# A windowed attention with an expert layer behind it: VectorE's operations between two SBUF tiles given to other engines, with a new list of steps

## The chip, the core and the metric

The kernel runs on one core of a Trainium2 chip. A core has TensorE (PE in the profile; its weight loads are PEld), VectorE (DVE), ScalarE (ACT), GpSimd (POOL) and SyncE (SP), which issues most DMAs. The metric is device time in microseconds (us), the median of several executions.

## The reference: what is computed

Two layers follow each other for a batch of 8 sequences of 576 tokens.

```python
# attention: 8 heads of 64, a symmetric window of 32 tokens on each side
scores = scale * np.matmul(q, k.transpose(0, 1, 3, 2))
mask = np.abs(pos[:, None] - pos[None, :]) <= window
scores = np.where(mask, scores, -1000000000.0)
...
x = softmax(scores) @ v            # heads side by side: (8, 576, 512)
# experts: 4 causal attention heads of 64, each with its own wq, wk, wv, wo
logits = x @ w_gate                # the 2 largest of 4, softmax over them: w
ye = softmax(causal(scale * (x @ wq[e]) @ (x @ wk[e]).T)) @ (x @ wv[e]) @ wo[e]
out = sum over the 2 chosen experts of w * ye
```

The inputs q, k and v are float32; the kernel computes the first layer's products in float32 and most of the second in bfloat16.

## The kernel before, in words

The work is a list of 967 steps, the string ORDER, written out in one line of text after another. A loop at the end of the kernel takes them one by one and calls the function of that name. The instructions of each engine run in the order of the list; between engines only data and buffers order them. A step is written as name and numbers, then after a colon the engine (v VectorE, g GpSimd, a ScalarE; for products of PE, p is whole and q is in halves of 64 rows of the result), then after @ the PSUM banks. So mk2011:g is the mask product of batch 2, group 0, half 1, pair 1, on GpSimd.

The steps of the first layer, by batch b and group g of four heads:

- lq, lk, lv load q, k and v. Each load is made to wait for the last PE instruction ahead of it in the list.
- tq and tk (line 317) turn q and k into tile T on VectorE, by a stream transpose from SBUF to SBUF. The first loads go another way: hq and hk turn them on PE, and iq and ik copy the result from PSUM into T.
- qc and kc copy one part of T to another place in T (line 184 when on VectorE or GpSimd, line 182 when on ScalarE), and mv moves further parts by four DMAs. There are 12 of each of the three: this doubles the rows of a product of q and k.
- sc multiplies q and k (line 190), ex takes the exponential out of PSUM into tile A (ScalarE, line 418), and mk multiplies A by the window's mask, tile MASKP (line 422). For batch 0 the mask is added on PE instead and there is no mk, so there are 56 mk steps.
- vc copies parts of v inside tile V. av multiplies A and V into PSUM, and un (lines 450 to 457, VectorE) divides into tile XN.
- xt turns XN on PE (line 193), xf copies that out of PSUM to XTF and xb casts XTF to XTB in bfloat16, both tiles in SBUF.

The steps of the second layer, by batch b and pair j of experts:

- ga, gt, ge, gm, gu compute the gate's weights (PE, then VectorE in lines 529 to 551, with one exponential on ScalarE).
- pp and pe compute q and k of the experts and cast them out of PSUM to QKE; pv and ve do this for v (VE).
- ps multiplies, xe takes the exponential into ATE (ScalarE, lines 618 and 620), se sets what is not causal to zero (GpSimd, line 623).
- po multiplies with v, oe (lines 657 to 659, VectorE) divides, applies the gate and writes OE; pt turns OE on PE (line 193), ot copies it to OTT.
- py multiplies with wo, ye copies to Y, st stores. For the last batch's last pair, pw, ow, tw and uw do po to ot in three parts.

lw0 to lw3 load the weights wq, wk, wv and wo, and cw0 to cw3 cast them. s_mask and s_nb build the masks at the start. The names after an arrow in the profile are tiles: A<-A,MASKP is a mask product, T<-T a qc or kc (or, as a DMA, an mv), XTB<-XTF an xb.

Tiles are few: A has three sets, T and V two each, XTF one, QKE and ATE three, OE two. A step that writes a tile waits until the readers of its last content are done.

Of the kernel before, what the change touches and what calls it, by code (L numbers as in the profile page):

```python
# [39 lines left out]
    lv23 un11@3 lq300:e av10@0 un10@0 cw2:a ex1111@5 mk1111:g pv01@7 lk300:e ve01:a@7 sc200@24 ex2001@4 ex2000@2  # L40
    sc201@06 ex2011@6 ex2010@0 tq210:e ps001:p@4 tk210:e xe001@4 xt10@2 lk310:e se013 mk1110:g xf10:a@2 ps000:p@6
    xe000@6 kc21:g lv20 av12@0 un12@0 av13@4 ps012:p@2 xe012@2 se001 un13@4 av14@0 un14@0 tq300:e qc21:g mv21
    ps002:p@6 lw3 xt11@4 xe002@6 se002 lv22 xf11:a@4 xt12@2 xf12:a@2 xb10:g xb12:g xb11:a pv00:p@0 ps003:q@4 ga1@2
    mk2010:g tk300:e ve00:a@0 xe003@4 lv21 se003 gt1 ge1 pp100:p@6 gm1 mk2001:g pe100:a@6 gu1@2 pp101:p@4
# [3 lines left out]
    ot01:v@7 pt00@6 xe100@0 pv10:p@4 ve10:v@4 ot00:a@6 lv31 mk2100:g ps113:p@0 ps110:p@2 xe113@0 mk2101:g xe110@2  # L48
    sc300@06 ex3000@0 sc301@24 ex3001@6 ex3010@2 pv11@0 py02@1 se101 ve11:a@0 ex3011@4 lq410:e vc21:g qc31:g
    ps112:p@6 mk2011:v xe112@6 mk2110:g vc20:g lv33 se103 av23@2 tq400:e un23@2 py01:q@4 se102 kc31:a mv31  # L50
    ps111:q@6 xe111@6 ye01:a@4 ye02:a@1 st02 tk400:e kc40:a se113 av24@0 se100 po10@2 oe10@2 mk3001:g av22@6 se110
    py00:q@4 pt10@3 qc40:a un24@0 st01 un22@6 ot10:v@3 se112 se111 po11@0 oe11@0 av20@6 ye00:a@4 st00 mk3010:g
    av21@4 un20@6 pt11@0 ot11:a@0 un21@4 mv40 sc310@26 ex3100@2 mk3011:g mk3000:v mk3100:g lk500:e sc311@04
    tq410:e ex3101@6 ex3110@0 ex3111@4 py11:q@2 lq500:e lv30 py12@7 ye12:a@7 xt20@0 ye11:a@2 xt21@4 lv32 xf21:a@4
    mk3111:g qc41:g py10:q@6 xf20:v@0 xb20:g xb21:g xt22@2 xf22:v@2 lv34 ye10:a@6 lv41 xb22:a sc401@04 ex4010@0
    mk4010:g tk410:e lv44 lk510:e sc400@26 ex4011@4 ex4000@2 pp200:q@0 pp201:q@2 ex4001@6 pp210:q@6 tk500:e
    pe200:a@0 pp211:q@0 pe201:a@2 kc41:a pe210:a@6 ga2@2 vc31:a mk3110:g ps202:p@6 tq500:e gt2 gm2 ps200:p@3
    pe211:a@0 mk3101:g av34@5 vc30:g av32@0 un34@5 ge2 gu2@2 un32@0 mk4011:g xe202@6 se202 mv41 xe200@3 qc50:a
    lq510:e av31@6 av30@2 pv21@0 un31@6 kc50:g mv50 mk4001:g ve21:a@0 av33@4 xt32@6 xf32:a@6 un30@2 mk4000:g lv43
    lv40 un33@4 xb32:a sc410@02 ex4101@2 sc411@46 mk4101:v lk600:e ex4100@0 tk510:e ex4111@6 mk4111:g xt30@2  # L60
    xf30:a@2 xt31@0 pv20:q@6 ve20:v@6 xf31:a@0 ex4110@4 lv42 ps212:q@0 xe212@0 sc501@24 ex5010@2 ex5011@4 lq600:e
    xb30:g mk4110:g sc500@06 xb31:g mk5010:g ex5000@0 ps211:q@2 xe211@2 pp300:p@4 lq610:e tq510:e pe300:v@4
    pp301:p@0 ex5001@6 ps203:q@2 ps201:q@4 lk610:e pe301:a@0 xe203@2 xe201@4 tk600:e qc51:g ga3@7 ps213:p@2
    xe213@2 ps210:p@0 ps302:p@5 xe210@0 xe302@5 gt3 kc51:g pp311:q@2 vc41:g pe311:a@2 vc40:g av43@0 mv51 pv31@6
# [24 lines left out]
    py42@6 ps601:q@4 st32 ps511:q@2 av74@7 un74@7 xe511@2 xe601@4 se601 av71@0 ye42:a@6 se511 un71@0 pp610:q@2
# [695 lines left out]
```

## Time and profile before

| | before |
|---|---|
| median of 3 runs | 252.7 us (249.24, 252.70, 253.34) |
| the profiled execution | 247.55 us |
| its span, first to last instruction | 245.7 us |
| mean granted clock of PE | 0.985 |
| DMA | 47.69 MB, mean 194 GB/s |

The profile is of one execution. Busy times of the engines overlap; a share of busy time is an average over stages with different limits. A row of a group ends with the idle time that its engine had just before these instructions and what ended it. In the timeline a row gives start, length, engine, line, operation, tiles and count; runs of equal instructions are merged into one row, and a bracket names the idle time ahead of it with what ended that. A row of a window gives its bounds, its length, the busy time of PE, PEld, DVE, ACT and POOL with their counts of instructions, the granted clock, the share of the DMA engines and GB/s.

### The profile page before, as it was taken

How to read it: one execution, taken by the hardware profiler on the slowest of the kernel's cores; microseconds unless marked ns; L12 is line 12 of the kernel's file. 1: busy time of each engine (PE TensorE's matmuls, PEld its weight loads, DVE VectorE, ACT ScalarE, POOL GpSimd, SP SyncE). 2: the span in 40 equal slices, each digit the busy share in tenths (PEclk: the TensorE clock that was granted, in tenths of full speed). 3: DMA queues.
4: the chain of work that ended last, by engine and by line, in shares of the span. 5: the costliest groups of instructions: out<-in, count | busy, mean ns of one | idle time of the engine just before them, and what ended most of it. 6: DMA issues, size and time to landing. Idle time of an engine off the chain costs nothing. (4 is left out here: it accounts for less than half of the span.)

```text
span 245.7 us, 11651 instructions
## 1 busy us (share of the span) xinstructions
PE 220.3 (90%) x5104; PEld 174.9 (71%) x5104; DVE 184.4 (75%) x326; ACT 165.6 (67%) x258; POOL 149.6 (61%) x195
## 2 busy tenths in 40 slices
PE   7989699999919999998998998999998799799991
PEld 3978576877806787987886876878786578567750
DVE  2551999799997998995896699877999776356651
ACT  2556268698815959986986895678658446677762
POOL 7003189648926956983998789298989623522310
PEclk9999999999976999999999999999999999999999
DMA  6889978898948689999997995894641403014555
GB/s 226 248 208 308 312 207 243 224 303 205 200 103 287 175 227 277 239 244 230 245 271 167 250 214 188 191 232 109 187 149 55 127 20 109 4 54 151 184 195 193
DMA packets 57107, 47.69 MB, mean 194 GB/s; under 512 B 40416, under 2 KB 42976, under 8 KB 57056
## 3 DMA queue, kind: packets, MB, share of 16 engines
q1 hardware_dynamic: 56480, 45.76, 68.1%
q10 hardware_dynamic: 576, 1.18, 1.3%
q8 instruction: 40, 0.66, 1.2%
q14 instruction: 11, 0.09, 0.1%
HBM read 30.42 MB, written 9.44 MB: 162 GB/s over the span
## 5 line engine op out<-in xcount | busy, mean ns | idle before, releaser
L422 POOL TENSOR_TENSOR A<-A,MASKP 128x576 f32<-128x576 f32 x46 | 65.5, 1435 | 12.6 <-ACT A L418 12.1
L618 ACT ACTIVATE ATE<-PS 128x1024 bf16<-128x1024 f32 x48 | 47.8, 1028 | 11.7 <-PE PS L190 11.4
L623 POOL TENSOR_SCALAR_AFFINE_SELECT ATE<-ATE 128x256 bf16<-128x256 bf16 (+1 forms) x80 | 29.8, 398 | 37.3 <-ACT ATE L618 28.3
L418 ACT ACTIVATE A<-PS 128x576 f32<-128x576 f32 x64 | 38.2, 654 | 12.6 <-PE PS L190 11.9
L190 PE MATMUL PS<-V,A 128*64 128x65 f32 (+1 forms) x1280 | 41.1, 223 | 2.4 <-issue 1.6
L190 PEld LDWEIGHTS PS<-V,A 128*64 128x64 f32 (+1 forms) x1280 | 37.0, 132 | 7.3 <-issue 3.7
L190 PE MATMUL PS<-T 64*64 64x128 f32 (+7 forms) x1440 | 39.5, 264 | 1.4 <-ACT XTF L182 0.6
L317 DVE STREAM_TRANSPOSE T<-kn 128x1152 f32<-128x1152 f32 x14 | 32.4, 2327 | 7.8 <-DMA kn<-in_k_dram 6.6
L190 PEld LDWEIGHTS PS<-T 64*64 64x64 f32 (+1 forms) x1440 | 33.7, 132 | 4.7 <-ACT XTF L182 0.8
L317 DVE STREAM_TRANSPOSE T<-qn 128x1152 f32<-128x1152 f32 x14 | 32.6, 2331 | 4.0 <-PE PS L190 3.1
L184 POOL COPY V<-V 64x2048 f32<-64x2048 f32 (+1 forms) x14 | 25.0, 1788 | 15.3 <-DMA V<-in_v_dram 14.2
L184 POOL CAST XTB<-XTF 128x1024 bf16<-128x1024 f32 (+1 forms) x25 | 16.5, 682 | 13.8 <-ACT XTF L182 12.8
L190 PE MATMUL PS<-QKE 64*64 64x64 bf16 (+9 forms) x252 | 18.9, 287 | 4.9 <-DVE OE L659 2.6
L451 DVE TENSOR_TENSOR XN<-PS,RC 128x512 f32<-128x512 f32 x32 | 22.1, 691 | 1.2
L182 ACT COPY XTF<-PS 128x1024 f32<-128x1024 f32 (+1 forms) x20 | 16.4, 828 | 9.6 <-PE PS L193 5.7
L182 ACT CAST QKE<-PS 128x576 bf16<-128x576 f32 x26 | 16.6, 643 | 7.8 <-PE PS L190 7.8
L190 PE MATMUL PS<-WV,XTB 128*128 128x256 bf16 (+2 forms) x208 | 19.8, 265 | 1.1 <-DVE XN L451 1.1
L182 ACT COPY Y<-PS 128x1024 f32<-128x1024 f32 (+1 forms) x20 | 16.2, 825 | 6.2 <-PE PS L190 3.6
L190 PE MATMUL PS<-WO,OTT 128*128 128x512 bf16 (+2 forms) x116 | 19.2, 352 | 0.7 <-DVE G L551 0.4
L190 PE MATMUL PS<-XTB,WQ 128*128 128x288 bf16 (+1 forms) x168 | 18.5, 287 | 0.1
L190 PE MATMUL PS<-XTB,WK 128*128 128x288 bf16 (+1 forms) x168 | 18.1, 287 | 0.0
L190 PEld LDWEIGHTS <-XTB 128*128 128x128 bf16 (+1 forms) x208 | 15.4, 107 | 3.6 <-issue 1.7
(88 smaller groups left out, 321.3 us busy)
## 6 DMA issues: line engine op xcount, KB each, us to landing
V<-in_v_dram SPq DMA_DIRECT2D x32, 256.0 KB, 5.4
out_dram<-Y SPq DMA_DIRECT2D x16, 512.0 KB, 3.9
qn<-in_q_dram SPq DMA_DIRECT2D x28, 288.0 KB, 4.6
kn<-in_k_dram SPq DMA_DIRECT2D x28, 288.0 KB, 5.0
T<-T SPq DMA_DIRECT2D x48, 144.0 KB, 4.3
V<-in_v_dram SPq DMA_DIRECT2D x8, 128.0 KB, 5.2
out_dram<-Y SPq DMA_DIRECT2D x16, 64.0 KB, 2.5
qn<-in_q_dram SPq DMA_DIRECT2D x2, 320.0 KB, 4.7
```

Source lines behind the costliest of these rows:

```text
L182: nc.scalar.copy(o, i)
L184: eng(c).tensor_copy(o, i)
L190: last_pe[0] = nc.tensor.matmul(*a, **kw)
L317: nc.vector.transpose(T.rearrange("q h (p o) -> q h o p", o=18)[:, :, o0:o1, :], x[:, :, o0:o1, :])
L418: nc.scalar.activation(AT[(2 * b + g) % NAT_][half][p], two(b0)[:, :, 0:HS], EXP, scale=scale_att)
L422: eng(c).tensor_tensor(out=ap, in0=ap, in1=MASK[:, None, HS * half:HS * half + HS].to_broadcast([128, 2, HS]), op=MULT)
L451: nc.vector.tensor_tensor(out=XN[T // 2][:, T % 2, :].rearrange("p (t h d) -> p h t d", t=4, h=8), in0=u[:, :, 0:64].rearrange("p h (d t) ...
L618: nc.scalar.activation(chunk(A, ch), two(b0), EXP, scale=scale_moe)
L623: nc.gpsimd.affine_select(ap, ap, pattern=[[0, n], [1, w]], compare_op=IS_GE, fill=0.0, base=0, channel_multiplier=-1)
```

## The change

The list of steps is replaced by another with the same 967 names. No function changes. In the new list no mk, qc, kc, vc, xb or cw step has the letter v:

| steps | before: v, g, a | after: v, g, a |
|---|---|---|
| mk | 10, 46, 0 | 0, 56, 0 |
| qc | 2, 7, 3 | 0, 8, 4 |
| kc | 0, 5, 7 | 0, 6, 6 |
| vc | 0, 14, 2 | 0, 13, 3 |
| xb | 1, 19, 4 | 0, 18, 6 |
| cw | 0, 2, 2 | 0, 3, 1 |
| iq and ik | 1, 0, 7 | 4, 0, 4 |
| xf | 7, 0, 17 | 10, 0, 14 |
| pe | 6, 0, 26 | 10, 0, 22 |
| ve | 5, 0, 11 | 7, 0, 9 |
| ot and uw | 9, 0, 9 | 8, 0, 10 |
| ye | 4, 0, 20 | 5, 0, 19 |

The stream transposes tq and tk and the mask set-up s_nb stay on VectorE. Steps in halves (q): pp 10 before and 12 after, ps 20 and 22, py 5 and 3, pv 1 and 0. The order and the banks of nearly all steps differ too, so the diff of the text is the whole string. Parts of it that the prediction speaks of:

```diff
-    lq001:e s_fill wm3@0 wm2@0 lq002:e s_warm s_ident lk001:f lq012:e lk002:f lk012:f lk011:f s_ones lv00 hq000@0
...
-    tq100:e lw1 hq010@0 iq010:a@0 lk100:e tk100:e lw0 hk010@4 cw0:g ik010:a@4 sc011@02 ex0110@0 sc010@46 lk110:e
...
-    pp011:p@4 pe011:a@4 lq210:e lw2 mk1000:g tq200:e qc20:g sc110@02 ex1100@0 ex1101@2 tk200:e kc20:a mk1010:g
...
-    pe101:a@4 lq310:e sc210@06 sc211@24 ex2101@6 kc30:g qc30:v mv30 ex2100@0 ex2110@2 se000 se011 pp110:q@6 se010
-    ex2111@4 lq400:e tk310:e se012 po01@2 oe01@2 pe110:a@6 ps103:p@4 cw3:a xe103@4 ps102:p@6 xe102@6 lk400:e
-    po00@0 pp111:p@4 oe00@0 mk2000:g lk410:e pe111:a@4 pt01@7 mk2111:g ps101:q@2 ps100:q@0 xe101@2 tq310:e
...
-    xe402@2 se303 mk5110:g av54@4 gm4 gu4@5 av53@0 un54@4 un53@0 qc70:g mv70 lk710:e av52@2 lv72 un52@2 xf50:a@6
...
-    xf62:v@2 ex7111@4 xb62:g xt60@6 xf60:v@6 xb60:v ex7110@0 xt61@4 xf61:a@4 sc710@02 ex7101@2 vc70:g xb61:g
+    lq012:e s_fill wm2@0 s_ones wm3@0 lk001:f lk002:f lq002:e lv03 lq001:e lk012:f s_ident hq011@0 iq011:v@0 lv00
+    hk000@7 ik000:a@7 s_mask s_nb lk011:f hk001@2 lk100:e ik001:a@2 hq001@0 lq011:e hq000@2 hk011@3 lv01 ik011:a@3
+    lv02 vc00:g lw2 iq001:v@0 iq000:v@2 sc001@06 sc000@24 tk100:e s_warm ex0011@6 ex0000@2 ex0010@0 hk010@6
...
+    tk200:e kc20:g xb00:a cw1:a lv14 lv10 ex1010@0 pp010:p@2 pe010:a@2 lv13 qc20:a pp011:p@4 pe011:a@4 lk210:e
...
+    pe111:a@2 pp110:p@0 se012 se001 po00@4 ps103:q@2 pe110:a@0 xe103@2 se010 mk2010:g tq300:e qc30:g mv30
+    ps102:q@0 xe102@0 lk400:e lv24 tk310:e kc31:a lq400:e po01@6 oe00@4 ps100:p@2 ps101:p@0 xe100@2 pv10:p@4 lv31
...
+    sc300@02 tk400:e ex3011@6 ex3010@4 py00:q@6 ex3000@0 vc21:g ex3001@2 mk2111:g mk2110:g av23@4 un23@4 ps113:q@2
...
+    se110 un24@7 se112 se111 vc30:a ye01:a@0 se113 po11@2 oe11@2 av21@4 un21@4 av20@0 un20@0 pt10@7 pt11@6 kc40:a
...
+    xt21@6 xf20:v@4 xb20:g py10:p@0 ye11:a@2 xf21:a@6 xb21:g xt22@2 sc401@46 ye10:a@0 ex4010@4 ex4011@6 xf22:v@2
+    sc400@02 xb22:a ex4000@0 lv34 lv41 mk3110:g qc41:g lv42 tk410:e tk500:e ga2@4 gt2 ex4001@2 pp200:q@6 lv43
...
+    tk510:e kc51:g pp300:p@6 pe300:v@6 vc40:g ex5000@0 mk5000:g pp301:p@2 pe301:a@2 tq600:e tk600:e
...
+    sc711@04 ex7110@0 st21 lv74 se501 ex7111@4 mk7001:g xt62@6 xf62:v@6 xt61@2 xf61:v@2 xt60@0 xf60:a@0 sc710@46
...
```

More of the change, by code (lines that the diff above doesn't have):

```diff
@@ L40 @@
[L40 to L44, printed above, removed]
@@ L50 @@
[L50 to L54, printed above, removed]
@@ L55 @@
[L55 to L64, printed above, removed]
@@ L95 @@
-    ps702:p@2 xe703@4 xe702@2 ps700:p@6 xe700@6 py51:p@4 pt60@0 ot60:a@0 st41 ye51:a@4 se611 po61@2 oe61@2 st52
-    st50 ga7@7 ps701:p@0 ps712:p@2 xe701@0 gt7 ge7 gm7 gu7@7 pt61@4 se703 ot61:a@4 xe712@2 st51 pv70:p@5 se701
-    py60:p@0 ye60:a@0 se702 py61:p@3 ye61:a@3 st60 st61 se712 ve70:v@5 pw710@7 ow710@7 se700 po70@5 py62@0 oe70@5
-    pw711@7 ow711@7 ps713:q@3 xe713@3 se713 ye62:a@0 st62 tw710@1 pt70@2 ot70:v@2 tw711@0 uw710:a@1 py70:p@1
-    uw711:a@0 py71:p@6 ye70:a@1 st70 ye71:a@6 pw712@0 st71 ow712@0 tw712@0 uw712:a@0 py72@0 ye72:a@0 st72
+    lq012:e s_fill wm2@0 s_ones wm3@0 lk001:f lk002:f lq002:e lv03 lq001:e lk012:f s_ident hq011@0 iq011:v@0 lv00
@@ new lines @@
+    sc100@46 xb01:g ex1001@6 ex1000@4 lv12 mk1001:g tq110:e sc101@02 tq200:e ex1011@2 wm1@7 mk1000:g mk1011:g
+    tk200:e kc20:g xb00:a cw1:a lv14 lv10 ex1010@0 pp010:p@2 pe010:a@2 lv13 qc20:a pp011:p@4 pe011:a@4 lk210:e
+    sc110@06 ga0@2 ex1101@6 gt0 mk1101:g ps010:q@6 gm0 pp000:p@4 pv01@3 pe000:v@4 ve01:v@3 ex1100@0 mk1100:g
+    vc10:g mv20 xe010@6 ge0 vc11:a gu0@2 lq210:e sc111@06 ex1111@6 tk210:e mk1111:g ex1110@0 mk1110:g kc21:g lv23
+    pp001:p@4 pe001:a@4 av10@2 un10@2 lv21 ps003:p@4 ps000:p@0 xe000@0 av11@6 lw3 un11@6 se000 ps011:p@2 xe003@4
@@ new lines @@
+    sc200@04 mk1010:g xe011@2 se011 ex2000@0 sc201@26 lk300:e lq300:e ex2001@4 mk2001:g ex2010@2 ps002:q@0 xe002@0
+    ex2011@6 tq210:e qc21:g mv21 av13@4 un13@4 av12@2 lv20 ps012:p@0 ps001:p@4 un12@2 xe012@0 av14@6 xe001@4
+    xt10@2 un14@6 se003 ps013:p@0 xe013@0 xt11@6 mk2000:g xf10:v@2 lk310:e xb10:g xt12@4 lv22 xf11:a@6 xb11:a
+    pv00:p@0 ve00:a@0 xf12:v@4 tk300:e kc30:a lv32 ga1@7 gt1 gm1 ge1 xb12:g pp100:q@5 pe100:a@5 se013 pp101:q@0
+    pe101:a@0 gu1@7 se002 sc211@24 ex2110@2 lq310:e sc210@06 cw3:g ex2100@0 mk2011:g ex2101@6 pp111:p@2 ex2111@4
@@ new lines @@
+    ex4110@4 lk600:e xt31@2 xf31:a@2 mk4110:g lv44 xb31:g tq510:e se200 qc51:g ex4111@6 pv20:p@0 ve20:v@0
+    ps212:q@2 xe212@2 sc501@46 ex5010@4 mk4111:g ex5011@6 vc41:g sc500@02 ex5001@2 lk610:e lq610:e ps211:q@4
+    xe211@4 tk510:e kc51:g pp300:p@6 pe300:v@6 vc40:g ex5000@0 mk5000:g pp301:p@2 pe301:a@2 tq600:e tk600:e
+    ps201:p@4 xe201@4 qc60:g ps203:p@0 xe203@0 ga3@7 gt3 se203 ps302:p@2 ps213:p@4 ps210:p@0 mk5001:g xe213@4
+    se213 pv31@6 pp311:q@4 xe302@2 xe210@0 mv51 av43@2 un43@2 av42@0 pe311:a@4 ge3 kc60:a mv60 ve31:a@6 pp310:q@4
@@ new lines @@
+    se300 mk5100:g po21@6 oe21@6 xe311@2 pp411:p@4 pp401:p@2 vc51:g qc70:a qc61:g pe411:v@4 ga4@0 pe401:a@2
+    ps403:p@4 ps401:p@6 kc61:a xe403@4 se403 ps310:p@1 xe401@6 mv61 xe310@1 pv41@3 tk700:e av51@4 lv61 av50@6
+    pt21@1 lv71 pt20@2 ot20:a@2 kc70:a st11 un51@4 ot21:a@1 gt4 un50@6 ve41:v@3 pv40:p@4 ge4 gm4 gu4@0 xt50@2
+    ps402:p@6 ve40:a@4 xe402@6 mk5111:g mk5011:g av54@1 mk6010:g av53@4 av52@6 xf50:a@2 un54@1 un53@4 ps313:q@2
+    mk6000:g mk6011:g xe313@2 xb50:g mv70 un52@6 sc610@04 st10 ex6100@0 sc611@26 tq710:e ex6101@4 se311 pp410:p@0
@@ new lines @@
+    av60@0 un61@3 ge5 gu5@2 un60@0 pe510:a@6 av63@6 un63@6 av62@2 pp511:q@0 un62@2 av64@7 pe511:a@0 mk7010:g
+    un64@7 ps410:q@2 xe410@2 mv71 lv70 sc711@04 ex7110@0 st21 lv74 se501 ex7111@4 mk7001:g xt62@6 xf62:v@6 xt61@2
+    xf61:v@2 xt60@0 xf60:a@0 sc710@46 ex7101@6 ex7100@4 se410 se413 ps412:q@2 pv50:p@0 xe412@2 se400 py20:p@4
+    ye20:a@4 se402 mk7000:g py31:p@2 ve50:v@0 po40@0 oe40@0 mk7111:g xb60:a ga6@4 ps500:p@5 ye31:a@2 xe500@5 gt6
+    ps510:p@0 xe510@0 gm6 se412 se411 po41@2 pt40@7 mk7100:g oe41@2 st22 xb61:g xb62:g pp601:p@5 pe601:v@5 ge6
@@ new lines @@
+    se512 se502 po50@4 oe50@4 se602 st31 xe611@0 py41:p@2 xb70:g ye41:a@2 st41 py40:p@6 ye40:a@6 ps610:p@0
+    ps612:p@4 se600 st40 se510 po51@2 xe610@0 oe51@2 xe612@4 xb72:g xb71:g pp711:p@6 pp710:p@0 pp700:p@4 pe710:v@0
+    se611 pe711:a@6 pe700:v@4 pt50@7 se601 ot50:a@7 pt51@0 se612 ot51:a@0 po60@2 oe60@2 ps613:q@4 xe613@4
+    ps711:q@6 ps710:q@0 xe711@6 xe710@0 se711 pp701:q@4 pe701:v@4 pv71@7 py52@6 se610 py50:q@2 st42 ye52:a@6
+    ve71:v@7 st52 ye50:v@2 ps703:q@4 st50 xe703@4 ps702:q@0 ps701:q@6 xe702@0 py51:p@4 ye51:v@4 se613 xe701@6
@@ L100 @@
+    po61@2 st51 ps712:p@0 oe61@2 xe712@0 se712 ps700:p@6 xe700@6 se700 se702 ga7@4 pt61@3 pt60@2 gt7 se701
+    ot60:a@2 se710 ge7 ot61:a@3 pv70:p@0 gm7 py60:p@2 py61:p@6 ye60:a@2 ve70:v@0 pw710@5 gu7@4 ow710@5 se703
+    po70@0 py62@2 oe70@0 ps713:q@4 st60 ye61:a@6 pw711@3 ow711@3 pt70@0 ye62:a@2 ot70:v@0 tw710@6 uw710:a@6
+    tw711@3 st61 uw711:v@3 py70:p@0 st62 xe713@4 py71:p@4 ye70:a@0 st70 ye71:a@4 st71 se713 pw712@7 ow712@7
+    tw712@7 uw712:a@7 py72@7 ye72:a@7 st72
 """
```

64 lines of the change are left out of this document (27 added, 37 removed).

## The prediction

> **What bounds the kernel now.** I read the page's head first, then PE's own waits, then the timeline around the two longest of them, then the groups of VectorE (DVE) and GpSimd (POOL).
>
> ```profile
> span 245.7 us, 11651 instructions
> PE 220.3 (90%) x5104; PEld 174.9 (71%) x5104; DVE 184.4 (75%) x326; ACT 165.6 (67%) x258; POOL 149.6 (61%) x195
> ...
> PEclk9999999999976999999999999999999999999999
> ```
>
> PE is busy 220.3 of 245.7 us, so what can be won by reordering is the other 25.4 us and whatever the low clock in slices 12 and 13 cost. PE's waits, longest first (total, times, longest):
>
> ```profile
> PE PS L193 <- DVE OE L659: 5.1, 1, 5.1
> PE PS L190 <- issue: 3.2, 4, 1.0
> PE PS L190 <- DVE OE L659: 2.6, 1, 2.6
> ```
>
> Two single waits, both for VectorE's OE, are 7.7 us. The timeline shows what VectorE did before them. First one:
>
> ```profile
> 61.67 7.97 DVE L184 COPY T<-T 128x576 f32<-128x576 f32 x1
> 62.01 1.84 POOL L623 TENSOR_SCALAR_AFFINE_SELECT ATE<-ATE 128x256 bf16<-128x256 bf16 x5
> 63.82 5.50 POOL L422 TENSOR_TENSOR A<-A,MASKP 128x576 f32<-128x576 f32 x4
> 69.56 2.32 DVE L317 STREAM_TRANSPOSE T<-kn 128x1152 f32<-128x1152 f32 x1
> 72.19 0.82 DVE L659 TENSOR_TENSOR OE<-PS,RG 128x640 bf16<-128x640 f32 x1
> 73.07 0.72 PE L193 MATMUL PS<-ident_bf,OE 128*128 128x128 bf16 x5 [5.09 <-DVE OE L659]
> 73.72 1.19 PE L190 MATMUL PS<-QKE 64*64 64x448 bf16 x12
> 75.34 3.09 PE L190 MATMUL PS<-WV,XTB 128*128 128x256 bf16 x16
> ```
>
> The copy of step qc30:v is on VectorE from 61.67 to 69.64, as long as POOL has selects and mask products queued back to back (62.01 to 69.32), and ends 0.3 us after the last of them. The transpose and two OE groups stand behind it; PE stands still for 5.09 us and then runs at half clock:
>
> ```profile
> 71.00:72.00 1.00, 0.00 (x0) 0.00 (x0) 0.96 (x3) 0.00 (x0) 0.00 (x0) 0.50 1.03 235
> 76.00:77.00 1.00, 1.00 (x6) 0.75 (x5) 0.74 (x2) 0.93 (x2) 0.97 (x1) 0.50 0.93 277
> ```
>
> (One-microsecond windows; the third figure from the end is the granted clock, 0.50.) The second wait follows a VectorE cast between two SBUF tiles (xb60:v), a third, smaller one a second T copy (qc61:v):
>
> ```profile
> 185.64 5.26 DVE L184 CAST XTB<-XTF 128x1024 bf16<-128x1024 f32 x1
> 187.22 2.78 POOL L422 TENSOR_TENSOR A<-A,MASKP 128x576 f32<-128x576 f32 x2
> 192.15 0.41 PE L190 MATMUL PS<-QKE 64*64 64x512 bf16 x4 [2.60 <-DVE OE L659]
> ...
> 150.10 2.37 DVE L184 COPY T<-T 128x576 f32<-128x576 f32 x1
> 153.37 1.91 PE L190 MATMUL PS<-WV,XTB 128*128 128x256 bf16 x16 [1.09 <-DVE XN L451]
> ```
>
> The same kinds of work on the engines that take them over, and VectorE's mask products (the last two rows give min/median/max in ns):
>
> ```profile
> L422 POOL TENSOR_TENSOR A<-A,MASKP 128x576 f32<-128x576 f32 x46 | 65.5, 1435 | 12.6 <-ACT A L418 12.1
> L184 POOL COPY T<-T 128x576 f32<-128x576 f32 x12 | 8.1, 686 | 3.8 <-DVE RC L450 2.7 <-DVE T L317 1.0
> L182 ACT CAST XTB<-XTF 128x1024 bf16<-128x1024 f32 x2 | 2.1, 1041 | 0.0
> L422 DVE TENSOR_TENSOR A<-A,MASKP 128x576 f32<-128x576 f32 x10 | 11.6, 1165 | 2.7 <-ACT A L418 2.7
> ...
> L422 DVE TENSOR_TENSOR A<-A,MASKP x10: 749/908/2249, 39.0 to 193.4; 128x576 f32<-128x576 f32 x10
> L422 POOL TENSOR_TENSOR A<-A,MASKP x46: 1396/1416/1947, 34.6 to 196.8; 128x576 f32<-128x576 f32 x46
> ```
>
> So a bound of PE, with holes that VectorE makes while it waits beside POOL.
>
> **The change part by part.** The program builds every computing instruction as before; engines, PSUM banks, halves (p or q) and places move.
>
> 1. *Off VectorE:* ten mask products (11.6 us), two T copies (7.97 and 2.37), one XTB cast (5.26): 27.2 us. *Onto VectorE, out of PSUM:* four iq evictions for one ik, four pe casts (0.758 each below) and five more small evictions on balance, about 9.6 us by the rows of VectorE's PSUM copies. VectorE ends near 184.4 - 27.2 + 9.6 = 167 us. ScalarE loses about 5 us; it is under 70% busy and ends no long wait of PE: nothing on the path.
>
> ```profile
> L184 DVE CAST QKE<-PS 128x576 bf16<-128x576 f32 x6 | 4.5, 758 | 3.7 <-PE PS L190 3.7
> L182 ACT CAST QKE<-PS 128x576 bf16<-128x576 f32 x26 | 16.6, 643 | 7.8 <-PE PS L190 7.8
> ```
>
> 2. *What of that is on the path.* The first wait: 5.09 us still, and after it work at half clock. The 16 matmuls of pv10 take 3.09 us there and 1.91 us at 153.37: 1.2; the ten of pt (0.72 us twice) and the twelve of ps (1.19) lose about 1.0 of their 2.63 by the same ratio: 7.3 us in all. The second wait 2.60, the third 1.09. Together 11.0 us. With the T copy gone the transpose starts at 61.7 and the OE groups find their matmuls done late (po01 begins at 65.9), so next in line is PE itself. I take all 11.0 as won; the bounds are 3.7 (only the two later waits go) and 11.0.
>
> 3. *Onto POOL:* ten products at 1.416 = 14.2, one more qc and kc each (0.67), one V copy and one XTB cast fewer, WV and WO's casts for WK's: about +13.9, to 163.5 us, 69% of a 236 us span. Spread out that is nothing; it isn't spread. From step se010 (PE's po00) to vc40 (before av43) the new list gives POOL 21 products (29.7), 8 T copies (5.3), 3 long and 2 short V copies (9.1), 11 wide and 2 narrow selects (5.2), 3 wide XTB casts and one pair of narrow ones (3.7): 53.0 us. The unit costs, and PE's work between the same steps in the trace:
>
> ```profile
> L184 POOL COPY V<-V 64x2048 f32<-64x2048 f32 x7 | 13.7, 1953 | 14.5 <-DMA V<-in_v_dram 14.2
> L184 POOL COPY V<-V 64x1536 f32<-64x1536 f32 x7 | 11.4, 1623 | 0.8 <-issue 0.7
> L623 POOL TENSOR_SCALAR_AFFINE_SELECT ATE<-ATE 128x256 bf16<-128x256 bf16 x64 | 25.4, 424 | 30.1 <-ACT ATE L618 28.3 <-issue 1.8
> L184 POOL CAST XTB<-XTF 128x1024 bf16<-128x1024 f32 x13 | 13.5, 1039 | 13.1 <-ACT XTF L182 12.8
> ...
> 65.91:126.21 60.30, 54.15 (x1254) 43.23 (x1254) 51.77 (x70) 43.79 (x72) 43.70 (x44) 0.94 0.84 222
> ```
>
> (In the 60.30 us from po00 to av43 PE was busy for 54.15 and POOL for 43.70.) Less the 2.2 of half clock, PE needs 52 us: POOL is full where it had air. At se010 the new list has POOL about 3 us ahead of PE (its work there waits only for xf12 and then runs through), and following the queues by the rows above, mk2110 is ready about 3 us before av23 needs it, se113 under 1 us before po11, xb21 about when pp200 starts, vc40 under 1 us before av43. Behind a late product stand selects and V copies, and for each of them PE. I charge 1.5 us; the bounds are 0 and a repeat of the first wait (7.3) at each of the three batches in the stretch, 21.9.
>
> 4. *Start.* WV's load (lw2) now goes out before WQ's and WK's, and V's block 3 before q's second part.
>
> ```profile
> Y<-in_moe_wv_dram SPq DMA_DIRECT2D x1, 512.0 KB, 6.9
> 24.00:30.00 6.00, 4.07 (x121) 3.40 (x120) 5.68 (x11) 1.00 (x3) 1.17 (x2) 1.00 1.07 309
> ```
>
> The queues are full then (share 1.07 at 309 GB/s), so 512 KB ahead of WK's load move that by 1.7 us. cw1 is on ScalarE's queue and pp011, pe010 and the exponentials of sc101 wait behind it. Against that PE's small waits for V and XN at 24 to 30 (1.9 us idle) are dealt anew. I charge +1.0, bounds -1 and +3.
>
> 5. *The rest of the list.* PE's other idle time is 25.4 - 5.09 - 2.60 - 1.09 = 16.6 us, much of it at start and end, which keep their shape (the last block is still pw712 to st72). The order of nearly every step differs, SP's too, where mv and the loads stay in pairs with their turns and place. I take the same 16.6 and give it 3 us either way. p and q halves cost the same: 16 half matmuls of pp 1.17 us, 8 whole ones 1.14.
>
> ```profile
> 63.43 1.17 PE L190 MATMUL PS<-XTB,WQ 128*64 128x288 bf16 x16
> 66.84 1.14 PE L190 MATMUL PS<-XTB,WK 128*128 128x288 bf16 x8
> ```
>
> Sum: -11.0 + 1.5 + 1.0 = -8.5 us. The profiled execution took 247.55 us (span 245.7), and would become 239.0. The median of the runs shown is 252.7 (249.24 to 253.34), 5.15 above the profiled one; I carry the difference over: 252.7 - 8.5 = 244.2 us.
>
> **The rivals.**
>
> *POOL gives the gain back in part.* One or two waits like item 3's bound. For: POOL's 53 us in 52. Against: most of its 61% share has idle time ended by ScalarE, not by itself. Two of 7.3: 252.7 - 11.0 + 14.6 = 256.3; one: 249.0. Within 2%.
>
> *POOL becomes the bound (other side).* In each of the batches 2, 3 and 4 PE waits for the mask product or the select of a queue that has lost its lead, long enough that the clock halves as it did at 71.00 (after about 3 us of standing). Three times 7.3 = 21.9, 252.7 - 11.0 + 21.9 = 263.6. It decides from the third such wait; two are not enough. For: the same full stretch; a product costs 1.4 on POOL and 0.75 on a free VectorE (the two rows of min/median/max). Against: in the stretch as I follow it nothing is over 1 us late. The Trainium skill, GPSIMD Engine Reference, Key points, has the rule that speaks for this rival: elementwise work is structurally about twice as fast on VectorE. By that rule ten products should not go to POOL at all; the trace agrees on the price, 0.749 against 1.396 us at the least.
>
> *The long copy is chance.* A blocked VectorE instruction gets in after one POOL instruction in most executions, and the 7.97 is an accident of this one. Then only 3.7 is won: 252.7 - 3.7 + 2.5 = 251.5. Against: 5.26 and 2.37 are over the copy's usual cost too, and the runs without a profile are longer, not shorter. The Trainium skill, SBUF — State Buffer, Who interferes with whom, has this rule: of a VectorE copy in a two-port mode and a GpSimd instruction, whoever issues first gets the shared ports for the whole instruction, and the other blocks. Taken at its word the copy waits for one instruction; in this trace it waited for ten.
>
> *The change does not do what it says.* Stream transposes still go from SBUF to SBUF on VectorE. They show no such wait:
>
> ```profile
> L317 DVE STREAM_TRANSPOSE T<-qn x14: 2316/2332/2341, 14.8 to 160.9; 128x1152 f32<-128x1152 f32 x14
> ```
>
> Fourteen within 25 ns, with POOL busy beside many; no chance of its own.
>
> **How the numbers follow.** 2% (5.05 us, about what a measurement of this kernel can tell from no change) puts the bounds at 247.65 and 257.75. The forecast, 244.2, has 0.62, its own range 236 to 247.6: below, all 11.0 won with no charge and no gap between profile and median (247.55 - 11.0 = 236.5); above, a charge of 6. POOL gives it back in part 0.13, the long copy is chance 0.07: both within 2%, 0.20. POOL the bound 0.18, slower. The range 236 to 257.7 holds all but that last case.
>
> **What would show it.** Right: no VectorE COPY, CAST or product with SBUF source other than the transposes and the mask set-up; VectorE near 167 us busy and POOL near 163; no wait of PE for OE over 2 us; PEclk 9 throughout; PE idle near 16 to 19 us. Item 3 wrong: PE waits ended by POOL A, POOL ATE or POOL V of over 1 us between 60 and 120 us. Item 4 wrong: ScalarE's WK cast ended by a DMA wait of over 2 us, with PE idle near 35 us. The forecast is wrong if the PEclk row shows a new dip.

## The result and the profile after

| | before | after |
|---|---|---|
| median of 4 runs | 250.97 us (248.91 to 253.34) | 237.19 us (234.73 to 238.82) |
| the profiled execution | 247.55 us | 234.73 us |
| its span | 245.7 us | 233.0 us |

The ratio is 0.949 [0.9351, 0.9629], and 0.9529 [0.9455, 0.9603] in a second measurement on another chip. Ratios here are of undisturbed executions only (within 1.5% of the fastest of the same kernel), so they differ a little from the quotients of the medians, and where too few are left none is given. The forecast was 244.2 us and faster: the sign held, the size is 13.8 us where 8.5 was expected.

The head of the changed kernel's page (busy time, share of the span and instructions of each engine, then the granted clock in 40 slices):

```profile
span 233.0 us, 11640 instructions
...
PE 216.2 (93%) x5089; PEld 174.4 (75%) x5100; DVE 168.2 (72%) x328; ACT 161.3 (69%) x246; POOL 158.9 (68%) x205
...
PEclk9999986999999999999999999999999999999998
```

The dip of the clock has moved from slices 12 and 13 to slices 6 and 7. PE's longest waits in the changed kernel:

```profile
PE PS L191 <- ACT A L419: 3.0, 1, 3.0
PE PS L191 <- issue: 2.2, 2, 1.9
PE PS L238 <- DVE ATE L233: 1.5, 1, 1.5
PE PS L194 <- DVE OE L699: 1.0, 2, 0.9
```

Neither of the two waits for OE of 5.1 and 2.6 us is left. The two longest now stand in the first 34 us. GpSimd's mask products, now all 56 (line, engine, operation, tiles, count: shortest, median and longest in ns, first and last start):

```profile
L423 POOL TENSOR_TENSOR A<-A,MASKP x56: 1399/1410/1432, 35.9 to 190.1; 128x576 f32<-128x576 f32 x56
```

With no product of VectorE beside them the longest is 1432 ns; before it was 1947.

Where the 12.7 us of span went is read from marks that both kernels have. The gate's exponential (EX<-L on ScalarE) runs once for each batch. I call its start in batch b gate b, and cut both executions at gates 0, 1, 2, 5 and 7. Columns: bounds, length, busy time of PE, PEld, DVE, ACT and POOL with their counts, granted clock, DMA share, GB/s. Before:

```profile
43.97:60.10 16.13, 15.41 (x412) 12.62 (x401) 14.26 (x24) 13.52 (x22) 10.10 (x15) 1.00 0.87 239
60.10:106.63 46.53, 41.23 (x924) 32.11 (x921) 41.89 (x53) 32.66 (x52) 34.88 (x38) 0.93 0.81 215
106.63:175.92 69.29, 65.79 (x1606) 54.70 (x1602) 56.04 (x98) 53.33 (x85) 54.62 (x64) 1.00 0.87 218
175.92:230.94 55.02, 50.38 (x1028) 39.40 (x1024) 38.85 (x85) 35.34 (x52) 27.66 (x46) 1.00 0.27 90
230.94:245.70 14.76, 9.11 (x112) 5.81 (x109) 5.97 (x20) 7.33 (x14) 2.55 (x7) 0.98 0.52 185
```

After:

```profile
45.20:63.95 18.75, 18.06 (x477) 14.96 (x478) 15.65 (x29) 15.12 (x22) 15.42 (x20) 1.00 0.87 239
63.95:102.20 38.25, 37.38 (x916) 30.40 (x914) 33.97 (x50) 31.66 (x51) 36.28 (x40) 1.00 0.95 259
102.20:168.39 66.19, 65.44 (x1591) 54.70 (x1590) 53.29 (x104) 52.95 (x83) 59.99 (x70) 1.00 0.80 221
168.39:218.25 49.86, 49.56 (x1021) 39.32 (x1022) 33.24 (x78) 35.59 (x51) 27.90 (x48) 1.00 0.35 113
218.25:233.00 14.75, 8.45 (x107) 5.54 (x107) 6.06 (x21) 6.12 (x12) 1.75 (x6) 0.92 0.46 164
```

Gate 1 stands at another place in the new list, so its two neighbours are added. The new list also places other work between the marks: 1060 matmuls are recorded ahead of gate 0 before and 994 after, 1333 and 1389 from gate 0 to 2. So between the two lists PE's idle time (length less busy time) tells more than the length. Between gates 5 and 7 PE of the changed kernel is busy for 49.56 of 49.86 us; before it stood still for 4.64 us there. The same cut for every kernel below (us, one profiled execution each):

| kernel | to gate 0 | 0 to 2 | 2 to 5 | 5 to 7 | to the end | span |
|---|---|---|---|---|---|---|
| before | 43.97 | 62.66 | 69.29 | 55.02 | 14.76 | 245.7 |
| b_copies_off | 43.54 | 57.25 | 67.63 | 58.24 | 15.14 | 241.8 |
| b_masks_off | 43.20 | 65.90 | 66.59 | 60.58 | 15.03 | 251.3 |
| b_all_off | 43.79 | 59.76 | 66.89 | 63.85 | 15.01 | 249.3 |
| b_copies_behind | 44.94 | 57.16 | 67.43 | 55.48 | 15.49 | 240.5 |
| b_all_mended | 43.92 | 58.60 | 67.83 | 55.27 | 14.98 | 240.6 |
| a_all_on | 44.43 | 62.44 | 66.52 | 50.62 | 14.69 | 238.7 |
| a_masks_on | 44.26 | 60.05 | 69.31 | 50.47 | 14.71 | 238.8 |
| a_copies_on | 44.65 | 59.58 | 66.96 | 50.00 | 14.71 | 235.9 |
| after | 45.20 | 57.00 | 66.19 | 49.86 | 14.75 | 233.0 |
| after_again | 45.26 | 58.80 | 67.35 | 49.87 | 14.72 | 236.0 |
| a_warm_first | 45.23 | 56.37 | 66.36 | 49.86 | 14.68 | 232.5 |
| a_wv_late | 45.64 | 56.46 | 65.79 | 49.86 | 14.75 | 232.5 |
| a_warm_wv | 43.58 | 57.88 | 66.23 | 49.87 | 14.84 | 232.4 |

The two executions of the changed kernel differ by 1.8 us from gate 0 to 2 and by 1.2 from 2 to 5, but by 0.01 from 5 to 7. Differences of that size in these two stretches are not read as effects.

### The profile page after: what moved, and what is told of

Read it like the earlier page. It is cut to its first block, busy times and chain, and to the rows that moved or that the text cites. A ratio compares the mean times of both kernels' runs of the same rounds, so it can differ in the third digit from the quotient of the medians.

```text
span 233.0 us, 11640 instructions
## 1 busy us (share of the span) xinstructions
PE 216.2 (93%) x5089; PEld 174.4 (75%) x5100; DVE 168.2 (72%) x328; ACT 161.3 (69%) x246; POOL 158.9 (68%) x205
## 5 line engine op out<-in xcount | busy, mean ns | idle before, releaser
L423 POOL TENSOR_TENSOR A<-A,MASKP 128x576 f32<-128x576 f32 x56 | 78.2, 1412 | 5.7 <-ACT A L419 5.4
L419 ACT ACTIVATE A<-PS 128x576 f32<-128x576 f32 x64 | 38.0, 652 | 14.2 <-PE PS L191 12.9
L191 PE MATMUL PS<-T 64*64 64x128 f32 (+7 forms) x1440 | 41.1, 275 | 2.6 <-issue 2.2
L191 PE MATMUL PS<-V,A 128*64 128x65 f32 (+1 forms) x1280 | 39.4, 222 | 0.6 <-DMA V<-in_v_dram 0.5
L185 POOL COPY V<-V 64x2048 f32<-64x2048 f32 (+1 forms) x13 | 22.0, 1696 | 14.1 <-DMA V<-in_v_dram 13.8
L183 ACT CAST QKE<-PS 128x576 bf16<-128x576 f32 x22 | 13.9, 644 | 7.5 <-PE PS L191 7.4
L191 PE MATMUL PS<-WV,XTB 128*128 128x256 bf16 (+1 forms) x192 | 18.6, 256 | 0.0
L183 ACT COPY XTF<-PS 128x1024 f32<-128x1024 f32 (+1 forms) x16 | 13.6, 855 | 7.3 <-PE PS L194 5.6
L191 PE MATMUL PS<-XTB,WQ 128*64 128x288 bf16 (+1 forms) x176 | 18.6, 289 | 0.0
L191 PEld LDWEIGHTS <-ATE 128*128 128x128 bf16 x480 | 16.3, 97 | 2.7 <-issue 0.9
L191 PE MATMUL PS<-XTB,WK 128*64 128x288 bf16 (+1 forms) x176 | 18.2, 286 | 0.0
```

The source lines that it names most:

```text
L183: nc.scalar.copy(o, i)
L185: eng(c).tensor_copy(o, i)
L191: last_pe[0] = nc.tensor.matmul(*a, **kw)
L419: nc.scalar.activation(AT[(2 * b + g) % NAT_][half][p], two(b0)[:, :, 0:HS], EXP, scale=scale_att)
L423: eng(c).tensor_tensor(out=ap, in0=ap, in1=MASK[:, None, HS * half:HS * half + HS].to_broadcast([128, 2, HS]), op=MULT)
```

## The experiments

Two questions. First: does the choice of engines alone make the gain (theory), or the order that came with it (rival)? Second: what do the new waits at the start cost? Kernels named b_ are edits of the list before, kernels named a_ of the list after.

### Engines changed in the old order

**b_copies_off**: the two T copies and the cast leave VectorE.

```diff
- kc30:g qc30:v mv30
+ kc30:g qc30:a mv30
...
- ps310:p@3 qc61:v pv41@2
+ ps310:p@3 qc61:a pv41@2
...
- xf60:v@6 xb60:v ex7110@0
+ xf60:v@6 xb60:a ex7110@0
```

> The list of before, with qc30, qc61 and xb60 alone moved from VectorE to ScalarE; the ten mask products stay on VectorE. Theory (VectorE's copies and casts between SBUF tiles wait for a gap in POOL's queue): the 5.09, 2.60 and 1.09 us waits of PE and the half clock after the first go, 250.97 - 11.0 = 240, between 237 and 244. Rival (the gain came from the new order and its spacing, not from the engine letters): within 2% of before, 246 or more.

Measured: 242.15 us (240.05 to 243.53), ratio 0.9801 [0.9709, 0.9892]. From gate 0 to 2 it takes 5.4 us less, where the forecast has 7.3: PE is idle there for 2.72 us (6.03 before) and busy for 54.53 (56.63 before). From 5 to 7 it takes 3.2 us more. The timeline there shows why (start, length, engine, line, operation, tiles, count, and the idle time ahead with what ended it):

```profile
175.89 2.22 DVE L184 COPY XTF<-PS 64x256 f32<-64x256 f32 x3
178.14 1.04 ACT L182 CAST XTB<-XTF 128x1024 bf16<-128x1024 f32 x1 [1.92 <-DVE XTF L184]
179.09 0.64 ACT L418 ACTIVATE A<-PS 128x576 f32<-128x576 f32 x1
179.79 2.11 PE L190 MATMUL PS<-T 64*64 64x64 f32 x40 [2.81 <-ACT A L418]
```

The cast xb60 has to wait for XTF, now on ScalarE's queue, and the exponential ex7110 stands behind it. PE waits 2.81 us for that exponential: the wait of 2.60 us for VectorE has become one for ScalarE.

**b_masks_off**: the ten mask products go to GpSimd, the copies stay. Ten edits of one kind:

```diff
- xe501@0 mk6100:v pp510:p@2
+ xe501@0 mk6100:g pp510:p@2
```

> The list of before, with only the ten mask products moved from VectorE to POOL; the three copies and casts stay on VectorE. Theory: the copies still wait, and POOL's queue ahead of them is at least as long: 249 to 255, with a T copy of 7 us or more at the same place. A second form of the theory (the products on VectorE block as much as the copies): 244 to 248. Rival (order): within 2% of before.

Measured: 253.72 us (252.0 to 257.88), ratio 1.0253 [1.0163, 1.0344]: slower. The T copies and the cast of VectorE in this kernel, the first copy with what GpSimd did beside it, and PE's two longest waits:

```profile
L184 DVE COPY T<-T x2: 473/4190/7908, 64.1 to 152.1; 128x576 f32<-128x576 f32 x2
L184 DVE CAST XTB<-XTF x1: 1586/1586/1586, 190.8 to 190.8; 128x1024 bf16<-128x1024 f32 x1
```

```profile
64.14 7.91 DVE L184 COPY T<-T 128x576 f32<-128x576 f32 x1
64.44 1.83 POOL L623 TENSOR_SCALAR_AFFINE_SELECT ATE<-ATE 128x256 bf16<-128x256 bf16 x5
66.25 5.48 POOL L422 TENSOR_TENSOR A<-A,MASKP 128x576 f32<-128x576 f32 x4
```

```profile
PE PS L193 <- DVE OE L659: 5.4, 1, 5.4
PE PS L190 <- POOL A L422: 5.3, 3, 4.0
```

The long copy repeats, 7.91 us beside 7.97, and so does PE's wait behind it. For this copy the rival that it was chance falls. The other two do not repeat, though they are still on VectorE: the second T copy takes 0.47 us (2.37 before), the cast 1.59 (5.26), and the waits of PE of 1.09 and 2.60 us behind them are not there. What GpSimd has queued at those two places is not the same in the two kernels. A new wait of 4.0 us for a product on GpSimd has come.

**b_all_off**: both edits together, so what the forecast's item 1 takes off VectorE, without any new order. (The two T copies go to ScalarE here, to GpSimd in the new list.)

> The list of before with both groups moved (copies and cast to ScalarE, ten products to POOL): the change of engines without the new order. Theory: most of the measured 13.8 us, 238 to 243. Rival (order): above 246. POOL as the bound, because this list was not laid out for ten more products: 244 to 250, with PE waits on A, ATE or V.

Measured: 250.89 us (249.76 to 251.9), ratio 1.0154 [1.007, 1.0238]. The engines alone gain nothing in the old order, and the theory of this run (238 to 243) falls. The stretch from gate 5 to 7 grows from 55.02 to 63.85 us: PE's idle time from 4.64 to 9.51, its busy time from 50.38 to 54.34 at a mean clock of 0.92. Two long waits stand there. The first in the timeline:

```profile
168.19 1.89 POOL L184 COPY V<-V 64x2048 f32<-64x2048 f32 x1
170.16 2.77 POOL L422 TENSOR_TENSOR A<-A,MASKP 128x576 f32<-128x576 f32 x2
173.38 2.76 POOL L422 TENSOR_TENSOR A<-A,MASKP 128x576 f32<-128x576 f32 x2
174.83 2.43 PE L190 MATMUL PS<-V,A 128*64 128x65 f32 x40 [4.02 <-POOL A L422]
```

PE starts av60 as soon as the first product of the row at 173.38, which is mk6100, is done; the V copies and the product mk7011, which is needed only for the next batch, ran ahead of it. The other wait is the same 2.81 us for ex7110 as above.

**b_copies_behind**: b_copies_off with xb60 one place later.

```diff
- xf60:v@6 xb60:a ex7110@0 xt61@4
+ xf60:v@6 ex7110@0 xb60:a xt61@4
```

> The kernel before with the three copies and the cast on ScalarE as in b_copies_off, and one thing more: the cast xb60 stands behind the exponential ex7110 in the list, not ahead of it. Theory (what an operation costs is its place in the queue of the engine that takes it): in b_copies_off ScalarE waited 1.92 us for XTF, made the cast (1.04) and only then ex7110, and PE waited 2.81 us for that and ran on at half clock. With ex7110 ahead that wait goes: the stretch from gate 5 to gate 7 falls from 58.2 to about 54 us, and the ratio to the kernel before from 0.980 to about 0.963 (239 us beside 248). Rival (the old order is loose as a whole, the next late thing takes the place): another wait of PE of over 2 us in the same stretch, the ratio stays between 0.975 and 0.985.

Measured: 241.69 us (238.26 to 246.35) beside 248.76, ratio 0.9699 [0.9599, 0.98]. No wait for ex7110 over 0.5 us is left, and the stretch is 55.5 us. The mechanism is shown; the size is smaller than expected (54 us) in the execution profiled, which took 242.26 us, and PE waits 1.57 us for an eviction into XTF at 181.27 instead. The ratio alone does not part theory and rival: its interval holds both figures.

**b_all_mended**: b_all_off mended at both places.

```diff
- xe502@4 vc60:g se400
+ xe502@4 vc60:a se400
...
- xe413@2 mk7011:g se413
+ xe413@2 se413
...
- xe501@0 mk6100:g pp510:p@2
+ xe501@0 mk6100:g mk7011:g pp510:p@2
...
- xb60:a ex7110@0 xt61@4
+ ex7110@0 xb60:a xt61@4
```

> The kernel before with all ten products on GpSimd and the copies and the cast on ScalarE as in b_all_off, mended at two places: xb60 behind ex7110, and of GpSimd's queue ahead of mk6100 the V copy vc60 given to ScalarE and mk7011 put behind mk6100. Theory (two places in the queues made the loss, 4.02 us for the late mk6100 and 2.81 us for the late exponential, each with half clock behind it): the stretch from gate 5 to gate 7 falls from 63.9 to about 54 us, the ratio to the kernel before from 1.015 to about 0.975 (242 us beside 248). Rival (GpSimd is short of time in the old order as a whole): PE waits over 2 us for another product, select or V copy of GpSimd, and the ratio stays at 0.995 or above.

Measured: 244.19 us (242.73 to 245.31), ratio 0.987 [0.9804, 0.9935], between the two expectations. PE's waits for GpSimd that are left:

```profile
PE PS L190 <- POOL A L422: 2.0, 3, 1.0
PE PS L190 <- POOL ATE L623: 1.5, 2, 0.8
```

None is over 1.0 us, and gate 5 to 7 falls by 8.6 us to 55.27. So two places in two queues made that loss, as the theory has it. But the ten products on GpSimd are still no gain in the old order: 0.987 beside 0.9699 with the copies alone. Where that difference arises the traces do not show; the profiled executions of the two kernels have spans of 240.6 and 240.5 us.

### Engines changed back in the new order

**a_copies_on**: qc30, qc61 and xb60 back to v, at their new places.

```diff
- tq300:e qc30:g mv30
+ tq300:e qc30:v mv30
...
- qc70:a qc61:g pe411:v@4
+ qc70:a qc61:v pe411:v@4
...
- mk7111:g xb60:a ga6@4
+ mk7111:g xb60:v ga6@4
```

> The new list with qc30, qc61 and xb60 put back on VectorE, nothing else changed. Theory: each of the three takes 2 to 8 us instead of 0.7 to 1, as POOL is 68% busy, and PE waits for what stands behind: 240 to 246. Rival (order): 237 within 1%.

Measured: 237.2 us (233.93 to 239.23), ratio 0.9533 [0.9405, 0.966], no difference from the changed kernel, so the theory (240 to 246) falls. The copies and the cast in it, and the longer copy with what GpSimd did beside it:

```profile
L185 DVE COPY T<-T x2: 449/1114/1778, 68.0 to 143.6; 128x576 f32<-128x576 f32 x2
L185 DVE CAST XTB<-XTF x1: 778/778/778, 186.5 to 186.5; 128x1024 bf16<-128x1024 f32 x1
```

```profile
67.98 1.78 DVE L185 COPY T<-T 128x576 f32<-128x576 f32 x1
67.98 3.53 POOL L185 COPY V<-V 64x1536 f32<-64x1536 f32 x2
```

At these places the three cost 3.0 us together (449 + 1778 + 778 ns), where they cost 15.6 before. The copy that costs 1.78 us there lies beside GpSimd's V copies, not beside a run of products; the one of 0.45 us begins at 143.61, and GpSimd does nothing from 143.70 to 146.08.

**a_masks_on**: ten mk steps back to v (mk1001, mk1011, mk1101, mk2011, mk3000, mk4101, mk6010, mk6100, mk7010, mk7110).

```diff
- oe31@6 mk6100:g lv72
+ oe31@6 mk6100:v lv72
```

> The new list with the same ten mask products put back on VectorE, nothing else. Theory formed after the first four runs (the order and spacing of the list carry the gain, the engine letters little): 235 to 240. Rival (a product of VectorE blocks as the copies did): 241 to 246, with VectorE products of 2 us and more.

Measured: 239.19 us (237.81 to 240.53), ratio 0.9643 [0.9564, 0.9723]. Its interval and those of the changed kernel touch; a loss of one or two per cent is likely, not settled.

**a_all_on**: the edits of a_copies_on and a_masks_on together, all thirteen back to v. The order, the banks and the other letters stay new.

> The new list with all thirteen steps back on VectorE (two T copies, the XTB cast, ten products): the new order without the change of engines. Theory (order): within 2% of the new list, 233 to 241. Rival (in the new list the engines matter after all, the two groups hurt together): 243 or more.

Measured: 240.99 us (240.58 to 241.48), ratio 0.9723 [0.9649, 0.9797]. This is the experiment that parts the two. The new list gains 2.8% with all thirteen on VectorE; taking them off gains about 2% more (0.9723 beside 0.9529 and 0.949). So neither the letters nor the order make the whole gain.

By stretch, a_all_on has the gain of 5 to 7: PE is idle there for 0.37 us, where it was 4.64 before. Of those 4.64, 2.60 were the wait for OE behind the cast and 1.55 a wait for XTF (at 211.36); both are gone with the order alone, and the cast, still on VectorE, takes 0.78 us at its new place. The gain of 0 to 2 is not there (62.44 us beside 57.00 and 58.80 in the changed kernel). In that stretch VectorE is full (rows in order of time):

```profile
66.13 1.66 DVE L423 TENSOR_TENSOR A<-A,MASKP 128x576 f32<-128x576 f32 x1
67.72 2.33 DVE L318 STREAM_TRANSPOSE T<-qn 128x1152 f32<-128x1152 f32 x1
68.22 3.42 POOL L185 COPY V<-V 64x1536 f32<-64x1536 f32 x2 [1.04 <-DMA V<-in_v_dram]
70.08 1.88 DVE L185 COPY T<-T 128x576 f32<-128x576 f32 x1
71.88 2.32 DVE L318 STREAM_TRANSPOSE T<-kn 128x1152 f32<-128x1152 f32 x1
...
74.50 0.82 DVE L660 TENSOR_TENSOR OE<-PS,RG 128x640 bf16<-128x640 f32 x1
...
75.38 0.82 PE L191 MATMUL PS<-WV,XTB 128*128 128x256 bf16 x6 [2.91 <-DVE OE L660]
```

A product and a copy, each held beside GpSimd for 0.9 and 1.4 us (1.66 and 1.88 less the 756 and 471 ns that such ones take at the median or at the least in this kernel), account for 2.3 of the 2.91 us that PE waits for OE. With the copy alone (a_copies_on) PE waits 1.2 us for OE at the most.

### The start

The changed kernel's first long wait, in the timeline:

```profile
14.47 2.34 DVE L318 STREAM_TRANSPOSE T<-kn 128x1152 f32<-128x1152 f32 x1 [2.86 <-PE PS L191]
16.75 0.07 DVE L226 MEMSET RC<- 128x8 f32 x1
16.85 0.21 ACT L227 ACTIVATE RC<-RC 128x8 f32<-128x8 f32 x1 [4.10 <-DVE RC L226]
16.97 1.17 ACT L419 ACTIVATE A<-PS 128x576 f32<-128x576 f32 x2
17.65 0.57 PE L191 MATMUL PS<-ident,kn 128*64 128x64 f32 x12 [2.99 <-ACT A L419]
```

The step s_warm, a memset on VectorE and a first exponential on ScalarE, has been put behind tk100. ScalarE stands for 4.10 us, the first exponentials of batch 0 wait behind that, and their bank is PE's next. The step has nothing left to warm up here: the kernel's only load of a function table (ACT_TABLE_LOAD, 1.28 us) is at 2.22 us in this list, ahead of a copy.

**a_warm_first**: s_warm moved right behind s_fill. **a_wv_late**: lw2 moved behind lw1 and cw2 behind mk1011:g. **a_warm_wv**: both. **after_again**: the changed kernel beside a_warm_wv.

```diff
- lq012:e s_fill wm2@0
+ lq012:e s_fill s_warm wm2@0
...
- tk100:e s_warm ex0011@6
+ tk100:e ex0011@6
```

```diff
- vc00:g lw2 iq001:v@0
+ vc00:g iq001:v@0
...
- av01@2 cw2:g ex0111@6
+ av01@2 ex0111@6
...
- lw1 un04@4
+ lw1 lw2 un04@4
...
- mk1000:g mk1011:g
+ mk1000:g mk1011:g cw2:g
```

> The new list with s_warm moved to its old place near the start, so that its memset no longer stands behind the transpose tk100 on VectorE. Theory: PE's wait of 2.99 us at 14.7 us goes and the span shortens by 2 to 3 us: 234 to 235. Rival (the start is bound by the loads, the wait comes back later): 236.5 to 238.

> The new list with WV's load after WK's and its cast (cw2) later on POOL. Theory (my charge of 1.0 us for the start, WQ and WK late by WV's 512 KB): 1 to 2 us faster, 235 to 236, and the 1.94 us wait of PE at 31.7 smaller. Rival (that wait is not for weights): no change, 236.5 to 238.

> The changed kernel again, beside its variants on one chip. Every theory expects the ratio of the result, 0.94 to 0.96, about 235.5 us beside 248; it is the measure for the next kernel.

> The new list with both edits of its start: s_warm right behind s_fill, and WV's load and cast late. Theory (each of the two made a stop of PE of its own, 2.99 us for s_warm and 1.94 us with the full DMA queues, and the half clock behind it): about 3 to 4 us less than the changed kernel on the same chip, a ratio of 0.930 to 0.940, and no stop of PE over 1.5 us before 42 us. Rival (the idle of the start is one bound, dealt anew by each edit: the single edits showed stops of 2.08 and 2.04 us at 36 to 40 us in place of the ones that they removed): within 1.5 us of the changed kernel on the same chip, 0.940 to 0.955, and a stop of about 2 us between 34 and 42 us.

Measured: a_warm_first 234.47 us (230.37 to 235.18), a_wv_late 234.79 (234.08 to 236.06; 0.9472 [0.9405, 0.9539]), both beside 247.93 before; after_again 235.63 (234.42 to 239.59) and a_warm_wv 233.86 (232.63 to 237.81; 0.9435 [0.9368, 0.9502]) beside 248.76. Without the late s_warm the wait of 2.99 us is gone, in a_warm_first and in a_warm_wv; in after_again it is there again. But PE in a_warm_wv:

```profile
38.00 0.77 PE L191 MATMUL PS<-XTB,WQ 128*128 128x288 bf16 x5 [2.43 <-issue]
```

That is the stop which the rival named; a_warm_first has one of 2.08 us at the same matmuls, and a_wv_late one of 2.04 in the same step, where the profile names a product of GpSimd as what ended it. The rival also put the time within 1.5 us of the changed kernel's; it is 1.8, with intervals that overlap, as that of a_wv_late does with the one of after_again. So the start's idle time is largely dealt anew by these edits. Whether a_warm_wv is better than the changed kernel is not settled. What the matmul of pp010 waits for at 38.00 the traces do not name, and the wait "issue" of 1.94 us at 33.66 in the profile of the result was 0.65 in after_again: it belongs to that execution.

## Why the prediction was right, and where it was off

**Item 1 (what moves).** VectorE 168.2 us where 167 was expected, ScalarE 161.3 (4.3 less, expected 5). GpSimd is 158.9 where 163.5 was expected, mostly because its own operations became shorter: the 56 products take 78.2 us (65.5 + 14.2 = 79.7 expected), the V copies 1.4 less (seven of 1893 ns where the prediction has 1953, six of 1466 where it has 1623), the wide selects 1.0 less (24.4 beside 25.4). It goes with VectorE's products: with only these taken away (b_masks_off) the longest product is 1439 ns and the short V copies take 1467 ns, with only the copies and the cast taken away (b_copies_off) 1934 and 1618.

**Item 2 (11.0 us on the path).** The mechanism is shown for the first wait: it repeats with the copy (b_masks_off) and goes with it (b_copies_off, 5.4 us from gate 0 to 2). Expected were 7.3, of which 2.2 for the half clock; PE's busy time fell by 2.1, but its idle time by 3.3 and not by 5.09. b_copies_behind has the same 5.5 less there; the kernel before was profiled only once, so the size is not settled closer. The second wait does not go by the letter: in the old order it changes engine, 2.60 for VectorE into 2.81 for ScalarE, and it is gone with the letter kept, in b_masks_off and in a_all_on. The step that failed is "next in line is PE itself", said of the first wait and summed for all three. After the second wait the next in line was the queue of the engine that took the cast.

**Item 3 (+1.5 for GpSimd's full stretch).** Not there: no wait of PE for GpSimd over 1 us, and from gate 1 to 2 PE is idle for 38.25 - 37.38 = 0.87 us. The rival "POOL gives the gain back in part" was a real danger all the same. It decides the old order, where one late product cost 4.02 us and what the copies had gained was lost again. The new list avoids it by what the forecast had counted only as load: vc60 on ScalarE, and products put where they are due.

**Item 4 (+1.0 at the start).** Gate 0 came 45.20 - 43.97 = 1.23 us later, with less of PE's work ahead of it; PE's idle time there grew by 2.3 us (7.86 beside 5.59), within the bounds. The mechanism did not hold. ScalarE's cast of WK was not held by its load, and without the early WV (a_wv_late) gate 0 is no earlier, 45.64 (with both edits of the start it is 43.58). The longest wait that the trace shows is behind s_warm, a step which I had not followed past tk100 on VectorE's queue. But with that wait gone and nothing else changed (a_warm_first) gate 0 is at 45.23, so what the 1.23 us come from stays open.

**Item 5 (the other 16.6 us of idle time unchanged).** The total held, its parts did not. PE's idle time by stretch (us; the second row takes the three waits of item 2 out of the first):

| | to gate 0 | 0 to 2 | 2 to 5 | 5 to 7 | to the end | sum |
|---|---|---|---|---|---|---|
| before | 5.59 | 6.03 | 3.50 | 4.64 | 5.65 | 25.4 |
| less 5.09, 1.09, 2.60 | 5.59 | 0.94 | 2.41 | 2.04 | 5.65 | 16.6 |
| after | 7.86 | 1.56 | 0.75 | 0.30 | 6.30 | 16.8 |
| after_again | 8.14 | 1.93 | 2.41 | 0.08 | 6.00 | 18.6 |

The new order took a further 1.7 to 2.0 us out of the stretch from gate 5 to 7, and the start gave 2.3 to 2.6 back. That the two nearly cancel is luck: the sum had 1.0 of the second and nothing of the first. Nor had it that the 2.60 us would go with the order and not with the letter of the cast. In the sum for the whole span the forecast had 16.6 us of idle time, 2.5 of charges and 220.3 - 2.2 = 218.1 us of busy PE, 237.2 us. The profile of the result has 233.0 us (16.8 idle and 216.2 busy), after_again 236.0 (18.6 and 217.4). So the sum was 1.2 to 4.2 us too long, and two executions of one kernel differ by 3.0.

**The signs.** As named: no wait for OE over 2 us, VectorE near 167 us, PE idle between 16 and 19 us. Not as named: a new dip of the clock, which was to show the forecast wrong, is there. In the changed kernel it begins within a stop of PE of 1.94 us (31.72 to 33.66), not after 3 us as at 71.00 before; in after_again it stands at another place. The first row is from the changed kernel, the second from after_again:

```profile
33.00:34.00 1.00, 0.34 (x12) 0.35 (x20) 1.00 (x2) 0.00 (x0) 0.55 (x1) 0.50 1.10 374
20.00:21.00 1.00, 1.00 (x21) 0.88 (x18) 0.00 (x0) 0.65 (x2) 1.00 (x1) 0.50 0.46 62
```

So the sign said nothing of the forecast: the place of the dip changes between executions of one kernel.

**The last step.** 5.15 us between profile and median were carried over from three runs; after it was 237.19 - 234.73 = 2.46. The miss of 7.0 us is 2.7 from that and 4.3 from the sum.

**The rule on elementwise work** that stood beside the rival "POOL becomes the bound" (the Trainium skill, GPSIMD Engine Reference, Key points) has the price right again: a product takes 756 ns on VectorE at the median in a_all_on and 1410 on GpSimd in the changed kernel. What follows for the time depends on the order. In the old one the move of the ten products cost 2.5% (b_masks_off); in the new one moving them back gains nothing (0.9643 beside 0.9529, with intervals that touch).

## What to carry to other kernels

An instruction that is moved off a busy engine is paid for at its place in the new engine's queue: look at what it has to wait for there, and at what stands behind it, before its duration is counted as won. Where an engine's letters and the order change together, cut both traces at marks they share and change one of the two at a time; here the new list without the thirteen letters gave 2.8%, and the letters without the new list a loss of 1.5%. Steps that carry no data, such as a warm-up of a function table, can hold the first link of a chain when they are put behind a long instruction.

## What the runs showed of the hardware

A VectorE copy between two SBUF tiles can be held for much longer than one GpSimd instruction. Beside five selects and four products back to back it took 7.97 and 7.91 us in two kernels, and it ended 0.3 us after the last of them. Beside two V copies of GpSimd it took 1.78 us (a_copies_on) and 1.88 us (a_all_on), about one of them, and 0.45 and 0.47 us where GpSimd stood idle. The Trainium skill, SBUF — State Buffer, Who interferes with whom, says that whichever of the two issues first has the shared ports for the whole instruction and the other blocks: that agrees with the V copies, not with the run of nine. Whether the kind of GpSimd's instructions or something else makes the difference was not tried.

The length of a single stop of PE does not tell whether its clock falls. The same stop of 2.99 us ended at 18.31 in after_again and at 18.14 in a_masks_on. Afterwards the clock was 0.50 from 20 to 21 us in the one and 1.00 in the other, and 1.00 also in the profile of the result, where the stop ended at 17.65.
